# Moving token sums, normalisations and GpSimd's rows around the start of each block of a fused attention and gated-MLP kernel

## The chip, the cores and the metric

The kernel runs on one core of one Trainium2 chip. The metric is the device time of one execution in microseconds. The kernel before was timed three times; the median counts. The profile is of one further execution.

## The reference

Eight batches of 576 tokens with eight heads of 64 go through linear attention without a softmax, a norm per head, and a gated MLP on all 4608 tokens:

```python
kv = np.einsum('bhsd,bhse->bhde', k, v)
out = np.einsum('bhsd,bhde->bhse', q, kv)
x = out / sqrt(mean(out * out, -1) + 1e-6) * g_norm       # then laid out as 4608 x 512
g, val = x @ w_gate, x @ w_val                            # 512 x 1536 each
ffn_out = (gelu(g) * val) @ w_out                         # 1536 x 512
result = x + sigmoid(x @ w_res) * ffn_out
```

## The kernel before

**Blocks.** The work is cut into nine blocks, counted from 0. Blocks 0 to 7 hold 512 tokens of batch 0 to 7; block 8 holds the 64 tokens that remain of each batch (the "remainders", 512 together). For each block the MLP is computed from x transposed, `xT`, and attention for a later batch runs between its products: while block m is at work, batch m + 2 gets its `kv`, its heads' products, sums of squares and its norm.

**Products by seven instead of eight.** Blocks 2 to 8 compute the gate (u = `g`) and value (u = `v`) products by a scheme of Strassen's kind: each is split into quadrants, and seven products stand for eight. `gv_group` does it for 512 of the 1536 columns; a block has three groups (i = 0, 1, 2). The scheme needs four sums of `xT`'s quadrants per block, the *token sums* `ts` 0 to 3 (`token_sums`, on VectorE). Products 5, 6, 7 and 4 take sums 0, 1, 2 and 3. One product is four matmuls of 128x256. The output product with `w_out` has the same shape (`out_by_products`, its products `w`), and so has the one with `w_res` (`res_halves`).

**The order is written out by hand.** There is a string of words for a group, and each engine executes its own instructions in the order in which the words issue them:

```python
ORDERS = {
    None: "1g 1v Eg 5g 6g Ev 5v dg 6v dv Fg 2g Fv 2v 7g g11 7v cg 3g cv 3v h11 g12 4g g21 h12 4v g22 h21 h22",
    False: "1g 1v Eg 5g Ev 5v dg 6g dv 6v Fg 2g Fv 2v 7g g11 7v cg 3g cv 3v h11 g12 4g g21 h12 4v g22 h21 h22",
```

A digit with a letter is a product on TensorE: 1 opens bank A, 5 opens bank F; 6, then 7, then 4 add to A; 2 adds to E, 3 to F. `E` is a copy of A into bank E (ScalarE), ahead of which 6 may not add to A. `d` is a copy of F to SBUF (ScalarE). `F` and `c` are VectorE's sums A + d, ahead of which 7 (after `F`) and 4 (after `c`) may not add to A. `g11` to `g22` are Gelu on ScalarE; `h11`, `h12` and `h21` are the products gate times value on VectorE, `h22` on GpSimd. The first groups of blocks 2 to 6 take the order `None`, other groups `False`; the last of a block has a third one.

**Work hung between the words.** `at_word(blk, i, word, f)` executes f behind a word of group i of block blk. `aside_out(blk, key, f)` executes f at a place of the output product of block blk; the keys come in the order `D`, `F`, `00`, `22`, `01`, `11`, `end`. What the change and the prediction's steps touch:

- `a_norm`: twelve small steps on GpSimd that give `ny`, 1 / rms, at place `F` of the output.
- `a_t(b, i)`: the normalisation of a quarter of a batch, `t<-op,ny` (VectorE, from the heads' product in PSUM bank i of four); i = 4 (`NJ`) is the remainder, `t<-o,ny`, from SBUF.
- `d_xT`: the transpose of `t` to `xT` by DMA, on SP's queue. `d_rem_qT` and `d_qT` transpose the next queries on the same queue.
- `a_g`: `xT` times g, in place, on VectorE (`xT<-xT,gcol`).
- `pf`: an output quarter times the gate, `osb<-th,w..`, on VectorE, or on GpSimd for one quarter. The last, `osb<-th,wA`, frees the bank that the next block's value product takes as E.
- `row_times_g`: GpSimd multiplies the block's four rows of `t` by g (`t<-t,g`) once `t` is not needed without g; `fin` adds them to the output (`osb<-osb,t`), and `store` writes it. `hold` is a copy of one element that keeps GpSimd from going on until what it reads is there.

**Banks.** The eight PSUM banks rotate. The first group of a block takes as F of its gate and value the banks that hold the heads' products 0 and 1, and the second group takes 2 and 3 as A. So 5g, 5v of the first group and 1g, 1v of the second wait for `a_t` 0 to 3.

Of the kernel before, what the change touches and what calls it, by code (L numbers as in the profile page):

```python
# [18 lines left out]
def kernel(  # L19
# [15 lines left out]
    nc = tc.nc  # L35
    P = nc.NUM_PARTITIONS
    B, H, S, D = q.shape
# [567 lines left out]
    def out_by_products(blk, banks, amid):  # L605
# [103 lines left out]
        def others():  # L709


            prod(w["A"], s_[1], wo_t[:, 1], False)
            aside("F")
            sub(nc.vector, w["F"], w["A"], w["d"], ALU.add)
            if res_and_attn(blk):
                s_last(blk)
            aside("00")
            prod(w["E"], a_of(blk, 1, 2), b_of(2, 1), False)
            if not whole(blk + 1):
                pf((0, 0), w["E"])  # L720
            aside("22")
            prod(w["A"], s_[2], wo_t[:, 2], False)
            c22 = res_all[part((1, 1))]
            sub(nc.vector, c22, w["A"], w["d"], ALU.add)
            if whole(blk + 1):
                pf((0, 0), w["E"])
            aside("01")
            prod(w["F"], s_[3], b_of(2, 2), False)
            pf((0, 1), w["F"])
            aside("11")  # L730
            prod(w["A"], a_of(blk, 2, 2), wo_t[:, 3], False)
            if whole(blk + 1):
                pf((1, 1), c22, nc.gpsimd)
                pf((1, 0), w["A"])
                aside("end")
            else:
                pf((1, 1), c22)
                pf((1, 0), w["A"])
            if blk + 1 == WHOLE or blk + 1 == LAST[0]:
                nc.gpsimd.tensor_copy(out=hold, in_=x_sums[blk + 1][0:1, 3, 1, 1, 0:1])  # L740
            if blk == LAST[0]:
                nc.gpsimd.tensor_copy(out=hold, in_=s_[3][0:1, 0, 0:1])
            for j in range(NJ):
                row_times_g(blk, j, nc.gpsimd)
# [3 lines left out]
            rows_behind()  # L748

        def rows_behind():  # L750

# [144 lines left out]
    def token_sums(blk, eng):  # L896
# [12 lines left out]
        ]  # L909

    ORDERS = {
# [3 lines left out]
    }  # L915

    def gv_group(blk, g, banks, amid, order):

        if blk not in hids:
            hids[blk] = hidp.tile([P, NF, NJ * P], FP16, tag="hid", name="hid")  # L920
# [61 lines left out]
            eng = nc.gpsimd if q == "22" else nc.vector  # L982
            eng.tensor_tensor(out=dst, in0=ge[q], in1=source(q, "v"), op=ALU.mult)  # L983

        for word in ORDERS[order].split():
# [12 lines left out]
            for f in amid.get(word, ()):  # L998
                f()
# [359 lines left out]
    def plan_attn_2():  # L1359
# [13 lines left out]
            at(m, 9 + j // 2, lambda j=j: a_t(b, j))  # L1373
        at(m, 10, lambda: d_xT(b, 0, NJ))
        for i in range(2):
            aside_out(m, "F", lambda i=i: a_g(b, 2 * i, 2 * i + 2))

    WHOLE = 2
    GROUPS = {blk: (1, 2) for blk in range(2, WHOLE)} | {blk: (0, 1, 2) for blk in range(WHOLE, B - 1)} | {B - 1: (1, 0, 2), B: (0, 1, 2)}
# [9 lines left out]
    def plan_attn_ahead(b):  # L1389
# [25 lines left out]
            at(m, NF - 1, lambda: a_kv(b, act))  # L1415
            at(m, NF, lambda: load_behind(b))
        if rem:
            at_word(m + 2, 0, "cv", lambda: a_g(b, NJ, NJ + 1))
            own = 2 * pair(b) + 1 == b
            at_word(m, last, "5v" if own else "3g", lambda: a_rem_kv(b))  # L1420
            at_word(m, last, "dv" if own else "g12", lambda: kv_out(b))
            if own:
                at_word(m, last, "3g", lambda: rem_mm(b))
            at_word(m, last, "g12", lambda: rem_out(b))
        else:
            at(m, NF, lambda: a_o(b), lambda: a_ss(b, 0), lambda: a_ss(b, 1))
            aside_out(m, "D", lambda: a_ss(b, 2), lambda: a_ss(b, 3))
        aside_out(m, "F", lambda: a_norm(b, 0, NJ + rem, pool))
        first = [lambda: new_block(b), lambda: a_t(b, 0), lambda: a_t(b, 1)]
        if whole(m + 1):  # L1430
            aside_out(m, "01" if m + 1 == WHOLE else "11", *first[0:2])
            amid_out[m].setdefault("end", []).insert(0, first[2])
        else:
            at(m, NF + 3, *first)
        if whole(m + 1):
            t = [lambda j=j: a_t(b, j) for j in range(NJ)]
            if rem:
                at_word(m + 1, 0, "h21", lambda: a_t(b, NJ), lambda: d_xT(b, NJ, NJ + 1))
            for i, word, fs in (
                (0, "1v", t[2:3]),  # L1440
                (0, "Fv", [t[3], lambda: d_xT(b, 0, NJ)]),
                (1, "cv", [lambda: a_g(b, 0, 2)]),
                (2, "Fv", [lambda: a_g(b, 2, NJ)]),
            ):
                at_word(m + 1, i, word, *fs)
# [18 lines left out]
    for blk in GROUPS:  # L1464
        t = token_sums(blk, nc.vector)
        if blk == 2:
            aside_out(blk - 1, "00", *t[0:2])
            aside_out(blk - 1, "end", *t[2:4])
            continue
        for key, f in zip(("00", "00", "22", "01") if whole(blk) else ("00", "22", "01", "11"), t):  # L1470
            aside_out(blk - 1, key, f)
    wr_ = wr_sums(nc.vector)
    at(0, NF + 1, *wr_[0:3])
# [42 lines left out]
    for blk in range(B + 1):  # L1516
# [21 lines left out]
        else:  # L1538
            slots = [lambda f=f: m_gval(blk, f) for f in range(NF)]
            groups = GROUPS.get(blk, ())  # L1540
            if groups:
# [6 lines left out]
                def group(i, blk=blk, ends=ends):  # L1548
                    if i == 0:
                        ends.extend(banks_of(blk))  # L1550
                        if blk + 2 < B:
                            o = att_at[blk]
                            pattn.opening = o[2:] + o
                    order = None if i == 0 and whole(blk) else i == len(GROUPS[blk]) - 1
                    gv_group(blk, GROUPS[blk][i], ends[i], amid_gv.get((blk, i), {}), order)

                for i in range(len(groups)):
                    slots[n + GF * i] = lambda i=i: group(i)
# [77 lines left out]
```

## Time and profile before

| | |
|---|---|
| median of 3 runs | 321.47 us (321.26 to 323.02) |
| profiled execution, whole | 321.97 us |
| its span, first to last instruction | 320.2 us |
| TensorE busy | 311.9 us (97%) |
| VectorE busy | 274.6 us (86%) |
| ScalarE busy | 210.8 us (66%) |
| GpSimd busy | 187.2 us (58%) |
| start of block 2, 3, 4, 5, 6, 7 | 91.59, 124.82, 157.34, 189.87, 222.60, 253.37 us |

The starts are those of each block's first product in the timeline. Busy time is the union of an engine's instructions; the end of a matmul is modelled, so two products in a row overlap in the records, and the time between their starts tells more than their ends. A timeline line has the start and the length in us, the engine, the line of the kernel, the operation, what it writes and reads, and in brackets the idle time ahead of it with what ended it. `x4` merges instructions in a row.

### The profile page before, as it was taken

To read this page: it belongs to the slowest core of one execution; us is meant where nothing else is said; L and a number is where in the kernel's file an instruction comes from. 1 tells how busy PE (TensorE), PEld (TensorE's weight loads), DVE (VectorE), ACT (ScalarE), POOL (GpSimd) and SP (SyncE) were. 2 spreads that over 40 slices of the span, in tenths; PEclk is the share of its full clock that TensorE was granted. 3 is DMA by queue.
4 is the path that set the end of the run, shared out by engine and by line. 5 is a ranking of instruction groups with operands and counts; after the bars stand their busy time and mean duration, and the time that the engine had idled before them with its cause. 6 is when DMAs were issued, how large, how long until landed. Compare 5 with 4: busy or idle time off the path is not lost.

```text
span 320.2 us, 7756 instructions
## 1 busy us (share of the span) xinstructions
PE 311.9 (97%) x3044; PEld 247.5 (77%) x3044; DVE 274.6 (86%) x486; ACT 210.8 (66%) x385; POOL 187.2 (58%) x249
## 2 busy tenths in 40 slices
PE   8989999999999999999999999999999999999993
PEld 3544755444788888888888888888888888888882
DVE  5788889799888899989998999799988777897774
ACT  3673684465847795878587858795768467836760
POOL 2792350572869378757875777517761375396332
PEclk9999999999999999999999999999999999999998
DMA  8999999799994899479947894800340003001204
GB/s 251 328 204 204 195 204 190 168 155 178 176 106 82 199 130 105 82 215 120 112 82 217 109 124 69 227 6 0 69 147 2 0 3 134 0 2 44 89 2 131
DMA packets 76694, 38.90 MB, mean 122 GB/s; under 512 B 42098, under 2 KB 74354, under 8 KB 76658
## 3 DMA queue, kind: packets, MB, share of 16 engines
q0 software_dynamic: 38752, 17.17, 42.4%
q1 hardware_dynamic: 37328, 20.71, 25.3%
q8 instruction: 24, 0.39, 0.5%
q10 hardware_dynamic: 578, 0.52, 0.5%
q14 instruction: 12, 0.10, 0.1%
HBM read 38.80 MB, written 9.44 MB: 151 GB/s over the span
## 4 chain that ended last, share of the span: by engine, by line
PE 96%; DVE 2%; issue 0%; ACT 0%; DVEq 0%
PE Av L946 12%; PE Ag L946 12%; PE wA L515 12%; PE Fv L946 6%; PE Fg L946 6%; PE gps L410 5%; PE vps L410 5%; PE rA L566 4%; PE fps L447 3%; PE Ev L946 3%; PE Eg L946 3%; PE wD L515 3%; PE wF L515 3%; PE wE L515 3%; PE w L515 2%; PE idle L1111 2%
## 5 line engine op out<-in xcount | busy, mean ns | idle before, releaser
L983 POOL TENSOR_TENSOR hid<-ge,c 128x512 f16<-128x512 f16 x22 | 25.6, 1162 | 40.2 <-ACT ge L977 40.2
L515 PEld LDWEIGHTS <-hid_s 128*128 128x128 f16 x384 | 37.6, 98 | 4.5 <-issue 0.2
L946 PEld LDWEIGHTS <-wsv 128*128 128x128 f16 x352 | 34.0, 98 | 5.6 <-issue 1.3
L946 PEld LDWEIGHTS <-wsg 128*128 128x128 f16 x352 | 34.4, 98 | 4.1
L361 POOL TENSOR_TENSOR t<-t,g 128x512 f16<-128x512 f16 x32 | 37.1, 1189 | 0.0
L702 POOL TENSOR_TENSOR osb<-osb,t 128x512 f32<-128x512 f32 x28 | 34.0, 1244 | 0.0
L956 ACT COPY Eg<-Ag 128x512 f32<-128x512 f32 x22 | 12.9, 585 | 27.8 <-PE Ag L946 27.8
L515 PEld LDWEIGHTS <-hid 128*128 128x128 f16 x288 | 28.2, 98 | 3.5
L946 PEld LDWEIGHTS <-wg 128*128 128x128 f16 x264 | 25.8, 98 | 3.2
L946 PEld LDWEIGHTS <-wv 128*128 128x128 f16 x264 | 25.8, 98 | 3.0
L946 PE MATMUL Av<-ts,wsv 128*128 128x256 f16 x176 | 26.4, 272 | 0.2 <-ACT Ev L956 0.2
L946 PE MATMUL Ag<-ts,wsg 128*128 128x256 f16 x176 | 26.4, 273 | 0.0
L967 DVE TENSOR_TENSOR Fg<-Ag,d 128x512 f32<-128x512 f32 x22 | 15.3, 696 | 12.3 <-ACT d L960 7.6
L258 DVE TENSOR_REDUCE ss<-sq 128x8 f32<-128x512 f32 x32 | 20.5, 679 | 1.7 <-ACT sq L253 1.7
L398 ACT ACTIVATE ge<-gps 128x512 f16<-128x512 f32 x20 | 11.8, 599 | 14.2 <-PE gps L410 14.0
L515 PE MATMUL wA<-wo_ts,hid_s 128*128 128x256 f16 x168 | 20.6, 273 | 0.0
L977 ACT ACTIVATE ge<-Eg 128x512 f16<-128x512 f32 x22 | 13.2, 598 | 10.0 <-PE Eg L946 10.0
L977 ACT ACTIVATE ge<-c 128x512 f16<-128x512 f32 x22 | 13.8, 627 | 7.8 <-DVE c L967 7.8
L345 DVE TENSOR_TENSOR t<-op,ny 128x512 f16<-128x512 f32 x28 | 18.4, 684 | 0.5 <-POOL ny L319 0.4
L977 ACT ACTIVATE ge<-Fg 128x512 f16<-128x512 f32 x22 | 13.0, 591 | 8.6 <-PE Fg L946 6.6
L967 DVE TENSOR_TENSOR c<-Ag,d 128x512 f32<-128x512 f32 x22 | 15.2, 689 | 4.1 <-PE Ag L946 4.1
L410 PE MATMUL gps<-xT,wg 128*128 128x512 f16 x72 | 18.5, 379 | 0.0
(219 smaller groups left out, 860.2 us busy)
## 6 DMA issues: line engine op xcount, KB each, us to landing
out_dram<-osb SPq DMA_DIRECT2D x14, 512.0 KB, 3.6
qraw<-in_q_dram POOLq DMA_DIRECT2D x7, 512.0 KB, 6.8
k<-in_k_dram POOLq DMA_DIRECT2D x7, 512.0 KB, 8.7
v<-in_v_dram POOLq DMA_DIRECT2D x7, 512.0 KB, 10.5
wg<-in_moe_w_gate_dram POOLq DMA_DIRECT2D x2, 512.0 KB, 8.4
wv<-in_moe_w_val_dram POOLq DMA_DIRECT2D x2, 512.0 KB, 8.8
wo<-in_moe_w_out_dram POOLq DMA_DIRECT2D x2, 512.0 KB, 13.9
out_dram<-osb SPq DMA_DIRECT2D x4, 256.0 KB, 4.5
```

Of the source, the lines that this page charges most:

```text
L258: nc.vector.tensor_reduce(out=out_, in_=sqs.pop((b, i)), op=ALU.add, axis=mybir.AxisListType.X)
L345: nc.vector.tensor_tensor(out=t, in0=o, in1=scale, op=ALU.mult)
L361: eng.tensor_tensor(out=t_t[blk][:, jj, :], in0=t_t[blk][:, jj, :], in1=g16, op=ALU.mult)
L410: nc.tensor.matmul(ps[:, j0 * P : j1 * P], lhsT=w[:, cc, :], rhs=xT_t[blk][:, j0:j1, cc, :], start=(cc == 0 and j0 == 0), stop=(cc == NP - ...
L515: nc.tensor.matmul(ps[:, e - es[0], :], lhsT=a[:, f, e * P : (e + 1) * P], rhs=b[:, f, :], start=(start and e == es[0] and f == 0), stop=( ...
L566: nc.tensor.matmul(out_[:, e, :], lhsT=x_[:, e, cc, :], rhs=w_[:, cc, :], start=(first and e == 0 and cc == 0), stop=(cc == 1), skip_group ...
L702: nc.gpsimd.tensor_tensor(out=res_all[of], in0=res_all[of], in1=t_t[blk][of], op=ALU.add)
L946: nc.tensor.matmul(out_[:, r, :], lhsT=lhsT, rhs=rhs, start=(first and r == 0 and c == 0), stop=(c == 1), skip_group_check=True,)
L956: nc.scalar.copy(out=tile_of("E", u), in_=ps["A", u])
L967: nc.vector.tensor_tensor(out=dst, in0=ps["A", u], in1=sb["d", u], op=ALU.add)
L977: nc.scalar.activation(out=ge[q], in_=source(q, "g"), func=AF.Gelu)
L983: eng.tensor_tensor(out=dst, in0=ge[q], in1=source(q, "v"), op=ALU.mult)
```

## The change

It rearranges five things. The token sums of blocks 3 to 6: sum 2 goes behind the last output quarter of the block before, sum 3 behind the word `Fv` of the block's first group. First groups get the common order of words. In the output stage the first two normalisations stand together ahead of the last output quarter; the fourth goes from `Fv` to `cv` of the first group, with the transpose of `xT` behind it, and in block 2 the third goes from `1v` to `Fv` and the first multiplication by g in the second group from `cv` to `h21`. GpSimd's four rows in the output of blocks 2 to 5 are issued at `Fv` of the next block, behind a `hold` on sum 3. The multiplication by g of remainders leaves the first groups of blocks 4 to 7 (one row each) and becomes two of two rows in block 7. In block 1's output, `xT` times g goes from place `F` to place `00`, behind the sum `wF`.

```diff
-            if blk + 1 == WHOLE or blk + 1 == LAST[0]:
-                nc.gpsimd.tensor_copy(out=hold, in_=x_sums[blk + 1][0:1, 3, 1, 1, 0:1])
-            if blk == LAST[0]:
-                nc.gpsimd.tensor_copy(out=hold, in_=s_[3][0:1, 0, 0:1])
+            if WHOLE < blk + 1 < LAST[0]:
+                at_word(blk + 1, 0, "Fv", rows)
+            else:
+                rows()
+            rows_behind()
+
+        def rows():
+            sums = s_[3][0:1, 0, 0:1] if blk == LAST[0] else x_sums[blk + 1][0:1, 3, 1, 1, 0:1]
+            nc.gpsimd.tensor_copy(out=hold, in_=sums)
             for j in range(NJ):
                 row_times_g(blk, j, nc.gpsimd)
...
-        None: "1g 1v Eg 5g 6g Ev 5v dg 6v dv Fg 2g Fv 2v 7g g11 7v cg 3g cv 3v h11 g12 4g g21 h12 4v g22 h21 h22",
...
-            aside_out(m, "F", lambda i=i: a_g(b, 2 * i, 2 * i + 2))
+            amid_out.setdefault(m, {}).setdefault("00", []).insert(i, lambda i=i: a_g(b, 2 * i, 2 * i + 2))
...
-            at_word(m + 2, 0, "cv", lambda: a_g(b, NJ, NJ + 1))
+            if b + 1 == B:
+                for i, word in ((0, "cv"), (2, "Fv")):
+                    at_word(LAST[0], i, word, lambda b=B // 2 + i: a_g(b, NJ, NJ + 2))
...
-            aside_out(m, "01" if m + 1 == WHOLE else "11", *first[0:2])
-            amid_out[m].setdefault("end", []).insert(0, first[2])
+            aside_out(m, "11", *first)
...
-                (0, "1v", t[2:3]),
-                (0, "Fv", [t[3], lambda: d_xT(b, 0, NJ)]),
-                (1, "cv", [lambda: a_g(b, 0, 2)]),
+                (0, "Fv" if first_whole else "1v", t[2:3]),
+                (0, "cv", [t[3], lambda: d_xT(b, 0, NJ)]),
+                (1, "h21" if first_whole else "cv", [lambda: a_g(b, 0, 2)]),
                 (2, "Fv", [lambda: a_g(b, 2, NJ)]),
...
-        for key, f in zip(("00", "00", "22", "01") if whole(blk) else ("00", "22", "01", "11"), t):
+        if whole(blk):
+            aside_out(blk - 1, "00", *t[0:2])
+            aside_out(blk - 1, "end", t[2])
+            at_word(blk, 0, "Fv", t[3])
+            continue
+        for key, f in zip(("00", "22", "01", "11"), t):
...
-                    order = None if i == 0 and whole(blk) else i == len(GROUPS[blk]) - 1
-                    gv_group(blk, GROUPS[blk][i], ends[i], amid_gv.get((blk, i), {}), order)
+                    gv_group(blk, GROUPS[blk][i], ends[i], amid_gv.get((blk, i), {}), i == len(GROUPS[blk]) - 1)
```

`first` is the new block's tiles, `a_t(b, 0)` and `a_t(b, 1)`; `first_whole` is true where m + 1 is block 2.

More of the change, by code (lines that the diff above doesn't have):

```diff
@@ L747, in others @@
                     row_times_g(B, p, nc.gpsimd)
-            rows_behind()
         def rows_behind():
@@ L915, with gv_group @@
     }
-    def gv_group(blk, g, banks, amid, order):
+    def gv_group(blk, g, banks, amid, last):
         if blk not in hids:
@@ L983, in hidden @@
             eng.tensor_tensor(out=dst, in0=ge[q], in1=source(q, "v"), op=ALU.mult)
-        for word in ORDERS[order].split():
+        for word in ORDERS[last].split():
             if word[0].isdigit():
@@ L1438, in plan_attn_ahead @@
                 at_word(m + 1, 0, "h21", lambda: a_t(b, NJ), lambda: d_xT(b, NJ, NJ + 1))
+            first_whole = m + 1 == WHOLE
             for i, word, fs in (
-                (0, "1v", t[2:3]),
-                (0, "Fv", [t[3], lambda: d_xT(b, 0, NJ)]),
-                (1, "cv", [lambda: a_g(b, 0, 2)]),
+                (0, "Fv" if first_whole else "1v", t[2:3]),
+                (0, "cv", [t[3], lambda: d_xT(b, 0, NJ)]),
+                (1, "h21" if first_whole else "cv", [lambda: a_g(b, 0, 2)]),
                 (2, "Fv", [lambda: a_g(b, 2, NJ)]),
```

## The prediction

> **What bounds the kernel now.** I read the page's parts 1 and 4 first, then the table of windows with one window per block, then the timelines of single groups, engine by engine. Blocks are counted from 0; a block starts at S, its first product of a first group.
>
> ```profile
> PE 311.9 (97%) x3044; PEld 247.5 (77%) x3044; DVE 274.6 (86%) x486; ACT 210.8 (66%) x385; POOL 187.2 (58%) x249
> ...
> PE 96%; DVE 2%; issue 0%; ACT 0%; DVEq 0%
> ```
>
> TensorE holds the end: 96% of the chain is its own work. Its instruction lists hold the same instructions before and after, so only its waits can change. Beyond 90 us I compared each product's start with the one before: a group of four matmuls (a "product") goes every 0.437 us, one of twelve every 1.31. The late ones are the stock that the change can gain from.
>
> ```profile
> 158.21 0.60 PE L946 MATMUL Fg<-ts,wsg 128*128 128x256 f16 x4
> 158.65 0.60 PE L946 MATMUL Ag<-ts,wsg 128*128 128x256 f16 x4
> 159.26 0.60 PE L946 MATMUL Fv<-ts,wsv 128*128 128x256 f16 x4
> ...
> 95.25 0.60 PE L946 MATMUL Ag<-ts,wsg 128*128 128x256 f16 x4
> 95.85 0.60 PE L946 MATMUL Av<-ts,wsv 128*128 128x256 f16 x4
> ...
> 106.79 0.60 PE L946 MATMUL Av<-ts,wsv 128*128 128x256 f16 x4 [0.20 <-ACT Ev L956]
> ```
>
> - Block 4, first group: 5v (Fv) starts 0.61 after 6g instead of 0.44, so 0.17 late. Blocks 3, 5 and 6 have the same at 126.74, 191.79 and 224.56 (0.17, 0.18, 0.17): 0.70 in all.
> - Block 2, first group: 95.25 to 95.85 is 0.60, and with 93.38, 95.25 and 97.63 it is 0.37 in all. Last group: 6v waits for ACT's Ev at 106.79; with 105.54 and 108.63 it is 0.51.
> - Block 1's output: a product of twelve starts at 86.19, the next at 87.67, 1.48 instead of 1.31: 0.17.
>
> Together **1.75 us** (0.54%) is all that the touched stretches can give back. A measurement of this kernel tells about 0.5%, 1.6 us, from no change.
>
> VectorE, ScalarE and GpSimd around the start of block 4:
>
> ```profile
> 156.44 0.49 POOL L318 TENSOR_SCALAR nh<-nh 128x40 f32<-128x40 f32 x1
> 157.02 0.27 POOL L319 TENSOR_TENSOR ny<-nh,ny 128x40 f32<-128x40 f32 x1
> ...
> 157.93 0.68 DVE L698 TENSOR_TENSOR osb<-th,wA 128x512 f32<-128x512 f32 x1
> 158.53 1.28 DVE L345 TENSOR_TENSOR t<-op,ny 128x512 f16<-128x512 f32 x2
> 159.81 0.70 DVE L967 TENSOR_TENSOR Fg<-Ag,d 128x512 f32<-128x512 f32 x1
> ...
> 158.70 0.57 ACT L956 COPY Ev<-Av 128x512 f32<-128x512 f32 x1
> 159.18 0.59 ACT L960 COPY d<-Fg 128x512 f32<-128x512 f32 x1
> ```
>
> 5v waits for the second normalisation (the first of the two at 158.53, ending 159.21): its bank held that head product. Ev starts 0.09 after osb<-th,wA ends, since it takes that bank. VectorE has no gap here.
>
> **What the skill says.** "SBUF — State Buffer", Who interferes with whom: a VectorE instruction with two SBUF inputs, or in a 2-port mode, and a GpSimd instruction that reads SBUF exclude each other for a whole instruction, and the earlier to issue wins; with one SBUF input VectorE doesn't contend. The trace agrees on the exclusion:
>
> ```profile
> 164.59 1.16 POOL L983 TENSOR_TENSOR hid<-ge,c 128x512 f16<-128x512 f16 x1 [1.61 <-ACT ge L977]
> 164.96 1.33 DVE L345 TENSOR_TENSOR t<-o,ny 128x512 f16<-128x512 f32 x1
> 166.22 0.69 DVE L967 TENSOR_TENSOR Fg<-Ag,d 128x512 f32<-128x512 f32 x1
> ...
> 103.40 1.49 DVE L370 TENSOR_SCALAR xT<-xT,gcol 128x1024 f16<-128x1024 f16 x1
> ...
> 103.45 1.15 POOL L702 TENSOR_TENSOR osb<-osb,t 128x512 f32<-128x512 f32 x1
> ```
>
> The remainder's normalisation t<-o (two SBUF inputs) ends 0.55 after the GpSimd instruction that it met (165.75), in block 3 too. Sums from PSUM (Fg, c, t<-op) keep 0.68 to 0.70 beside GpSimd. On who wins, the trace adds a warning: at 103.40 g on xT, recorded 0.05 ahead of GpSimd's next add, lost to it and ended 0.28 after that add's end (104.61).
> "Perfetto Trace Analysis", Identifying the Most-Contended Engine, holds matmul busy time to be a poor measure; hence the products' starts above.
>
> **The change, part by part.** Read with block 4; blocks 3, 5 and 6 repeat its times to some 0.02.
>
> 1. *Sums 2 and 3 leave the output stage.* Beside them two of GpSimd's small steps for ny took 0.49 and 0.32, where the like take 0.29 or less and 0.24. So ny comes 0.3 earlier, at 157.0 instead of 157.29. Bounds: 0 (VectorE was not the cause) and 0.45, where osb<-th,wF (at 156.25 then) holds the first normalisation.
> 2. *Both normalisations ahead of osb<-th,wA.* At VectorE's step of 0.60: t 157.0 and 157.6, wA's at 158.2. The second t ends at 158.3, ahead of 5v's new turn (158.65): the 0.17 goes. Late next is Ev: 158.2 + 0.68 + 0.09 = 158.97, ending 159.54. In the common order 6v follows 6g, its turn is S + 5 x 0.437 = 159.52, and with 0.05 from ScalarE to TensorE it starts at 159.59, 0.07 late. Then d (ends 0.505 after Ev), Fg at 160.08, Fv 160.68 to 161.37, so 7v at 161.42 against its turn of 161.27: **0.15 late in place of 0.17**, a draw. Bounds, from step 1's: 0 and 0.45.
> 3. *Third sum at the last output, fourth behind Fv, t 3 behind cv, no g on the remainder.* VectorE loses 0.34 x 2 earlier and gets it here, less the g (0.26). The sums are needed by 7g and 4g, whose turns are later than their ends (159.2, 161.7). t 3 ends at 163.5; 1v of the next group, its first user, is due at 164.0. The transpose of xT moves with it from 161.88 to about 163.6 on SP; at the 4.3 to landing of the page it is there at 168, g on it follows at about 169. The remainder's transpose, qrT and qT behind it on SP move by under 1 us; their users are at 174 and later.
> 4. *GpSimd's rows behind the fourth sum*, four of 1.15 (1.11 apart), with one more 0.18 hold per block. They start 3.5 later; hid (h22) of the group ends at 167.9 instead of 165.75, for c of the next group needs it by 168.2, so it stays hidden. The four adds and the stores behind them move by 2 us; the next hid is used at 176.9. Queued behind the hold are only these.
> 5. **Where rows and t<-o meet.** The fourth sum starts 0.60 after Fv, 161.28, and ends at 161.70. Behind it VectorE has c, c, t, three hid: t<-o's turn is 0.34 + 6 x 0.597 = 3.92 after the sum's start, 165.20. GpSimd: hold 0.06 after the sum, first row 0.15 later (both as at 94.06), the fourth 3.34 after that: 165.25; the third ends at 165.29. This is the pattern of 103.40, 0.05 ahead and lost. I take it as lost: the fourth row ends at 166.41, t<-o at 166.96, Fg of the second group runs 166.88 to 167.57, 7g starts at 167.62 against a turn of S + 22 x 0.4366 = 166.95; Fv ends at 168.16, 7v starts at 168.21 against 167.38. The block is then **0.83 late**, 0.66 more than now. Both chains hang on the same sum, so the four blocks should agree: 4 x 0.66 = +2.6. Bounds for t<-o itself: 0.69 (free) and 1.7 (a whole row, and 0.55).
> 6. *Block 2 and block 1's output.* With g on xT behind wF, wF reads A at 86.55 instead of 86.92: -0.17. The first group gets its two t early, Ev ends before 6v's turn: -0.37, with about 0.03 left at 4v. With g on xT behind h21 in the second group, h12 comes 1.4 earlier and so does Ev of the last: -0.51. Sum **-1.0**.
> 7. *Block 7.* g on 1024 elements twice for 512 once: 0.48 against 0.34 at cv, and 0.48 in the last group at Fv, where VectorE idles 0.45 ahead of c. TensorE had no late product there, VectorE 1.1 idle in the second group: nothing.
>
> Sum: -1.0 + 2.6 = +1.6. The profiled execution took 321.97 (span 320.2 and 1.8 around it), so 323.6 on its scale; it lies 0.5 above the median of 321.47, on whose scale I forecast **323.1**.
>
> **Rivals.**
> - *t<-o gets the port after the third row.* It then ends at 165.84, the fourth row waits instead, and 7g has 0.4 to spare. For it: the record puts t<-o 0.05 ahead, and the skill lets the earlier one win. Against it: 103.40. First groups -0.1, block 2 -1.0: **320.4**, not slower. It decides at 0.05: anything that makes t<-o 0.1 earlier against the rows.
> - *Lost, and ny no earlier.* Ev, the sum and t<-o all come 0.3 later against TensorE: 0.3 x 4 more, **324.3**. Against it: the 0.49 beside a sum.
> - *Port won and ny earlier by 0.4.* No late product is left in first groups: -1.0 - 0.7, **319.8**.
> - *The change doesn't do what it says*: the order of instructions shows every move, so this has no share.
>
> **Numbers.** Lost port 0.48 (322.5 to 323.7; a little over half lies above 323.08, since stalls not seen can only add), lost with late ny 0.21, won 0.23, won and all gone 0.08. Slower by over 0.5%: 0.27 + 0.21 = 0.48; faster 0.08; within 0.44. The range reaches from the won case to the late one, 320.1 to 324.4.
>
> **What would show it.** t<-o of 1.7 in blocks 3 to 6 and 7g of the second group about 0.5 late: step 5 right; t<-o of 0.7: the first rival. 6v late by under 0.1: step 2. ny at S - 0.3: step 1. No late product in 85 to 110 us: step 6. A late first product of a group, or hid on GpSimd holding c, would make the reading wrong.

## The result, and the profile after

The changed kernel takes **354.41 us** (median of 4 runs, 354.07 to 356.27), against 321.50 us for the kernel before on the same chip. The ratio is **1.102 (95% interval 1.098 to 1.107)**: 33 us slower, where 1.6 were forecast. The profiled execution took 354.48 us, with a span of 352.5.

The page of the kernel after: busy times, the granted TensorE clock in 40 slices, the chain by engine, and two groups of part 5 (busy time, mean ns of one, idle time ahead and what ended it).

```profile
PE 320.7 (91%) x3044; PEld 251.5 (71%) x3044; DVE 298.0 (85%) x484; ACT 210.0 (60%) x385; POOL 184.0 (52%) x253
...
PEclk9999999999999997899969999699978999999999
...
PE 78%; DMA 10%; issue 7%; DVE 1%; SPq 1%; POOL 0%; DVEq 0%
...
L950 PE MATMUL Ag<-ts,wsg 128*128 128x256 f16 x176 | 28.1, 285 | 23.6 <-DVE Fg L971 23.6
...
L345 DVE TENSOR_TENSOR t<-o,ny 128x512 f16<-128x512 f32 x4 | 29.2, 7292 | 0.0
```

The clock line of the kernel before:

```profile
PEclk9999999999999999999999999999999999999998
```

Four instructions t<-o take 7.29 us each (1.33 to 1.58 before), TensorE stands 23.6 us before `Ag` for `Fg`, and its clock, full before, dips at four places. The same in one block, the timelines of VectorE, GpSimd and TensorE in block 3:

```profile
131.22 7.29 DVE L345 TENSOR_TENSOR t<-o,ny 128x512 f16<-128x512 f32 x1
...
127.92 4.49 POOL L361 TENSOR_TENSOR t<-t,g 128x512 f16<-128x512 f16 x4
132.38 1.15 POOL L987 TENSOR_TENSOR hid<-ge,c 128x512 f16<-128x512 f16 x1
133.49 4.47 POOL L702 TENSOR_TENSOR osb<-osb,t 128x512 f32<-128x512 f32 x4
...
132.68 0.60 PE L950 MATMUL Ev<-xT,wv 128*128 128x256 f16 x4
139.18 1.01 PE L950 MATMUL Ag<-ts,wsg 128*128 128x256 f16 x4 [5.89 <-DVE Fg L971]
139.98 1.06 PE L950 MATMUL Av<-ts,wsv 128*128 128x256 f16 x4
```

t<-o stands until GpSimd's adds end (137.96) and ends 0.55 behind them, at 138.51. `Fg` follows, and 7g starts at 139.18 instead of 133.12, 6.06 late. From there to 144.0 a product of four takes 0.85 instead of 0.44: 23 matmuls take 4.81 us where they would take 2.51, 2.3 us more.

| block, start to start | 2 | 3 | 4 | 5 | 6 | 7 |
|---|---|---|---|---|---|---|
| before, us | 33.23 | 32.52 | 32.53 | 32.77 | 30.74 | 30.57 |
| after, us | 32.37 | 40.94 | 40.96 | 41.19 | 39.04 | 30.81 |
| difference | -0.86 | +8.42 | +8.43 | +8.42 | +8.30 | +0.24 |

The differences add up to 32.95, about the whole result: four blocks that each lose 6.06 + 2.3, and small change beside them. (The trace before has the start of block 6 at 222.64, 0.04 later than in the list of starts further up.)

The first group of block 4 and the last of block 2 in the kernel after, to set against those shown in the prediction:

```profile
165.97 0.60 PE L950 MATMUL Ag<-ts,wsg 128*128 128x256 f16 x4
166.55 0.60 PE L950 MATMUL Av<-ts,wsv 128*128 128x256 f16 x4
...
167.86 0.60 PE L950 MATMUL Ag<-ts,wsg 128*128 128x256 f16 x4
168.39 0.60 PE L950 MATMUL Av<-ts,wsv 128*128 128x256 f16 x4
...
104.91 0.60 PE L950 MATMUL Ag<-ts,wsg 128*128 128x256 f16 x4
105.35 0.60 PE L950 MATMUL Av<-ts,wsv 128*128 128x256 f16 x4
```

In block 4, 6v starts 0.58 after 6g instead of 0.44 and 7v 0.53 after 7g: 0.14 and 0.09 late. In block 2, 6v follows 6g by 0.44, where it was 0.37 late before.

### The profile page after: what moved, and what is told of

Read it like the earlier page. It is cut to its first block, busy times and chain, and to the rows that moved or that the text cites. A ratio compares the mean times of both kernels' runs of the same rounds, so it can differ in the third digit from the quotient of the medians.

```text
span 352.5 us, 7758 instructions
## 1 busy us (share of the span) xinstructions
PE 320.7 (91%) x3044; PEld 251.5 (71%) x3044; DVE 298.0 (85%) x484; ACT 210.0 (60%) x385; POOL 184.0 (52%) x253
## 4 chain that ended last, share of the span: by engine, by line
PE 78%; DMA 10%; issue 7%; DVE 1%; SPq 1%; POOL 0%; DVEq 0%
PE Ag L950 12%; PE Av L950 11%; PE wA L515 10%; PE Fv L950 6%; PE Fg L950 6%; DMA wo<-in_moe_w_out_dram 4%; PE rA L566 4%; PE gps L410 3%; PE fps L447 3%; PE vps L410 3%; PE wE L515 3%; PE wD L515 3%; PE wF L515 3%; DMA wg<-in_moe_w_gate_dram 3%; PE w L515 2%
## 5 line engine op out<-in xcount | busy, mean ns | idle before, releaser
L950 PEld LDWEIGHTS <-wsg 128*128 128x128 f16 x352 | 35.6, 102 | 29.5 <-issue 24.3
L950 PE MATMUL Ag<-ts,wsg 128*128 128x256 f16 x176 | 28.1, 285 | 23.6 <-DVE Fg L971 23.6
L950 PEld LDWEIGHTS <-wsv 128*128 128x128 f16 x352 | 35.7, 102 | 6.8 <-issue 0.3
L702 POOL TENSOR_TENSOR osb<-osb,t 128x512 f32<-128x512 f32 x28 | 31.4, 1147 | 0.0
L950 PEld LDWEIGHTS <-wg 128*128 128x128 f16 x264 | 26.7, 101 | 4.1
L950 PEld LDWEIGHTS <-wv 128*128 128x128 f16 x264 | 26.6, 101 | 3.8
L345 DVE TENSOR_TENSOR t<-o,ny 128x512 f16<-128x512 f32 x4 | 29.2, 7292 | 0.0
L950 PE MATMUL Av<-ts,wsv 128*128 128x256 f16 x176 | 28.2, 286 | 0.0
```

Of the source, the lines that this page charges most:

```text
L345: nc.vector.tensor_tensor(out=t, in0=o, in1=scale, op=ALU.mult)
L702: nc.gpsimd.tensor_tensor(out=res_all[of], in0=res_all[of], in1=t_t[blk][of], op=ALU.add)
L950: nc.tensor.matmul(out_[:, r, :], lhsT=lhsT, rhs=rhs, start=(first and r == 0 and c == 0), stop=(c == 1), skip_group_check=True,)
```

## The experiments

At the start stood two theories. One: GpSimd keeps VectorE out for as long as its instructions that read SBUF follow each other, a *run* (here rows, hid and adds). The other: a waiting t<-o is let in at the next end of a GpSimd instruction if it was asked well before that end, and here it came a trifle too late each time. Every edit but one is made to the kernel after. "Asked 0.3 ahead" means that the recorded start of the VectorE instruction lies 0.3 us before that of GpSimd's next.

### A break in the run, and an earlier asking

`gap` puts a memset of one element behind the fourth row. `t_at_h12` issues t<-o one place, 0.6 us, earlier.

```diff
             for j in range(NJ):
                 row_times_g(blk, j, nc.gpsimd)
+            if WHOLE < blk + 1 < LAST[0]:
+                nc.gpsimd.memset(spare, 0.0)
...
-                at_word(m + 1, 0, "h21", lambda: a_t(b, NJ), lambda: d_xT(b, NJ, NJ + 1))
+                at_word(m + 1, 0, "h12", lambda: a_t(b, NJ), lambda: d_xT(b, NJ, NJ + 1))
```

> The changed kernel with one GpSimd memset of a single element, which reads nothing, behind the fourth row of blocks 2 to 5. Port theory (what starves t<-o is that each next GpSimd instruction that reads SBUF already stands at the port): the memset leaves the port free for a moment, t<-o is served behind the fourth row, about 1.8 us long, TensorE about 0.6 late in each block, about 323.7 us. Rival (GpSimd keeps the port as long as it is busy at all, or t<-o waits for something else): t<-o stays at 7.3 us and the time at 354.

> The changed kernel with the remainder's normalisation t<-o (and its transpose) at the word h12 instead of h21 of the first group: it asks for the port one VectorE step, 0.60 us, earlier, about 0.64 ahead of the fourth row's start, in the middle of the third row. Handover theory (an instruction that asks within some 0.05 us of the change from one GpSimd instruction to the next loses to every GpSimd instruction that follows without a gap; one that asks in the middle of an instruction is served at its end): t<-o takes about 1.2 us, no long wait of TensorE, no half clock, about 321.7 us. Rival, the run (t<-o loses to the whole run of rows, hid and adds whenever it meets it, whatever the moment): t<-o takes about 7.9 us and the time stays at 354 or above.

Measured: gap **324.19 us**, t_at_h12 **357.07** (one execution each, the kernel before 322.89). VectorE, GpSimd and TensorE in block 3 of gap:

```profile
131.81 1.73 DVE L345 TENSOR_TENSOR t<-o,ny 128x512 f16<-128x512 f32 x1
...
132.94 0.09 POOL L752 MEMSET spare<- 1x1 f32 x1
133.00 1.57 POOL L989 TENSOR_TENSOR hid<-ge,c 128x512 f16<-128x512 f16 x1
...
134.21 0.60 PE L952 MATMUL Ag<-ts,wsg 128*128 128x256 f16 x4 [0.33 <-DVE Fg L973]
134.81 0.60 PE L952 MATMUL Av<-ts,wsv 128*128 128x256 f16 x4
```

A memset of 0.09 in each of four blocks takes back 30 of the 33 us. t<-o gets in at 132.94, hid waits for it (1.57 instead of 1.15), and TensorE's clock does not dip. 7g and 7v start 0.50 and 0.16 late; with the 0.23 of the first group the block is 0.89 late, where the forecast had 0.83 (and 1.7 for t<-o) for a row lost *once*. The first t<-o of t_at_h12:

```profile
131.14 7.90 DVE L345 TENSOR_TENSOR t<-o,ny 128x512 f16<-128x512 f32 x1
```

It is asked 0.64 ahead of the fourth row, as are the other three, and all take 7.9: asked well inside a row t<-o still loses the run, so the second theory falls in this form.

### Other times of asking

`rows_later` makes GpSimd's copy ahead of the rows once to four times more in blocks 3 to 6, `t_later` puts one to four VectorE memsets ahead of t<-o, `scan` mixes both for places between.

```diff
-            nc.gpsimd.tensor_copy(out=hold, in_=sums)
+            for _ in range(blk if WHOLE < blk + 1 < LAST[0] else 1):          # rows_later
+                nc.gpsimd.tensor_copy(out=hold, in_=sums)
...
-                at_word(m + 1, 0, "h21", lambda: a_t(b, NJ), lambda: d_xT(b, NJ, NJ + 1))
+                at_word(m + 1, 0, "h21", *[lambda: nc.vector.memset(spare, 0.0)] * (b - 3), lambda: a_t(b, NJ), lambda: d_xT(b, NJ, NJ + 1))   # t_later
...
+            for kind in {3: "hhm", 4: "hhmm", 5: "m", 6: "mm"}.get(blk + 1, ""):  # scan: h the copy, m a memset
+                if kind == "h":
+                    nc.gpsimd.tensor_copy(out=hold, in_=sums)
+                else:
+                    nc.gpsimd.memset(spare, 0.0)
...
-                at_word(m + 1, 0, "h21", lambda: a_t(b, NJ), lambda: d_xT(b, NJ, NJ + 1))
+                at_word(m + 1, 0, "h21", *[lambda: nc.vector.memset(vspare, 0.0)] * (3 if b > 4 else 0), lambda: a_t(b, NJ), lambda: d_xT(b, NJ, NJ + 1))
```

> The changed kernel with 1, 2, 3 and 4 further hold copies ahead of the rows in blocks 3, 4, 5 and 6, which move the rows and all behind them about 0.24 us later for each; t<-o then asks about 0.29, 0.53, 0.77 and 1.0 us ahead of the fourth row. Handover theory: served at the third row's end, about 0.87, 1.11, 1.35 and 1.6 us long, about 321.5 us. Rival, the run: 7.5 to 8.3 us each, 354 or above.

> The changed kernel with 1, 2, 3 and 4 memsets of a single element on VectorE ahead of t<-o in blocks 3, 4, 5 and 6, some 0.06 us each (they write one element and read nothing), so t<-o asks about 0.02, 0.08, 0.14 and 0.2 us behind the recorded start of the fourth row. Handover theory: block 3 still starves (7.2 us) or is served once; blocks 5 and 6, and likely 4, are served at the fourth row's end, about 1.6 us; about 330 us or 323. Rival, the run: about 7.2 us in all four, 354.

> The kernel after with t<-o's asking set to four places within a running row: block 3 about 0.54 us after the start of the third row, block 4 about 0.49 after it (GpSimd's rows begin later by two copies of one element and one or two memsets), block 5 about 0.27 and block 6 about 0.21 after the start of the fourth row (three VectorE memsets ahead of t<-o, one or two GpSimd memsets ahead of the rows). Theory C, a request is kept only if it is made late enough in the running instruction (third row: 0.47 lost and 0.59 was served; fourth row: 0.20 lost and 0.32 was served): each of the four is either served at the next end (block 3: 1.1 to 1.2 us; block 5: 1.4) or lost for the whole run (7 to 8 us), later ones served and earlier ones lost, block 3 more likely served than 4 and 5 more than 6. Rival D, the outcome has nothing to do with the time of asking within the row: no order, for instance block 4 served and block 3 lost. The total is about 321.5 plus 8.4 for each that is lost.

Measured: 339.13, 347.05 and 329.77 us, one execution each. (In scan block 4 got the three VectorE memsets too, so t<-o was asked 0.67 after the third row's start there, not 0.49.) The twelve t<-o of these traces, with the time by which they were asked ahead of GpSimd's next instruction:

| GpSimd's next | asked ahead, us: t<-o took, us |
|---|---|
| fourth row | 0.28: 0.86; 0.44: 1.02; 0.52: 1.10; 0.54: 1.12; 0.77: 8.02; 0.99: 8.23; 0.04: 7.29 |
| hid | 0.79: 1.37; 0.92: 7.05; 0.95: 7.08; 1.03: 7.17; 1.08: 1.67 |

Each is let in at the first end after it was asked, or not until GpSimd idles; nothing lies between. Each lost run costs some 8.4 us of the total. From 0.28 to 0.54 ahead all were let in, from 0.77 most were lost, but not in order (0.79 and 1.08 were let in): the rule that `scan` was to test, that only the time of asking decides, does not hold at its long end.

### A break too early, and other kinds of instruction

`open_row4` puts the memset ahead of the fourth row instead of behind it. `kind` puts one more VectorE instruction at t<-o's place (`h21`), ahead of it, of another kind in each block.

```diff
+                if j + 1 == NJ and WHOLE < blk + 1 < LAST[0]:                    # open_row4
+                    nc.gpsimd.memset(spare, 0.0)
                 row_times_g(blk, j, nc.gpsimd)
...
+        if b == 4:                                                               # kind, blocks 3 to 6
+            nc.vector.tensor_tensor(out=out, in0=g16, in1=g16, op=ALU.add)
+        elif b == 5:
+            nc.vector.tensor_scalar(out=out, in0=g16, scalar1=gcol, scalar2=None, op0=ALU.mult)
+        elif b == 6:
+            nc.vector.tensor_tensor(out=out, in0=o, in1=o, op=ALU.add)
+        elif b == 7:
+            nc.vector.tensor_tensor(out=out[:, 0:256], in0=o[:, 0:256], in1=o[:, 256:512], op=ALU.add)
```

> The kernel after with one GpSimd memset of one element ahead of the fourth row in blocks 3 to 6. Theory A, GpSimd keeps the port as long as its instructions that read SBUF follow each other, and a memset between them opens it: t<-o asks about 0.1 us ahead of the row, is served at the memset, takes 0.65 to 0.9 us instead of 7.29, 7g of the second group is at most 0.1 late and TensorE's clock does not dip. What is left of the change is then block 2 (-0.86), first groups (0.23 instead of 0.17, +0.06 four times) and block 7 (+0.24): 321.5 - 0.4 = 321.1. Theory B, a memset opens the port only for a request that was already waiting when it began: t<-o comes 0.05 too late for it, loses to the row and all that follows, 7.2 us, and the time is 354.

> The kernel after with one more VectorE instruction ahead of t<-o, so asked for 0.04 ahead of the fourth row, another kind in each block: block 3 a sum of two fp16 tiles of 128x512 in SBUF (as a token sum), block 4 an fp16 tile times a column (as g on xT), block 5 a sum of fp32 and fp32 without broadcast, block 6 the same on 128x256. It fills t's remainder, which t<-o then overwrites. Theory E, whether a VectorE instruction loses a run depends on the time of asking alone: all four take over 7 us, as t<-o did there. Theory F, it depends on the kind (in the runs so far fp16 sums and g on xT lost one GpSimd instruction at most): the fp16 ones of blocks 3 and 4 take 1.4 to 1.6 us, the fp32 ones of blocks 5 and 6 over 7. In either case t<-o behind it meets the rest of the run and may lose it.

Measured: open_row4 **348.15 us** (346.72 to 354.04), kind 355.71. In open_row4 the memset begins 0.01 to 0.03 after t<-o's recorded start, and t<-o loses the run in three of four blocks of the trace (7.32 to 7.33; in the fourth it is let in behind the fourth row, 1.76). The recorded start of t<-o overlaps the end of the instruction before it by 0.08, so it may not have been waiting yet (not shown). The timeline of VectorE in kind, the inserted instruction of each block:

```profile
131.35 7.03 DVE L351 TENSOR_TENSOR t<-g 128x512 f16<-128x512 f16 x1
...
173.03 6.89 DVE L353 TENSOR_SCALAR t<-g,gcol 128x512 f16<-128x512 f16 x1
...
214.29 7.30 DVE L355 TENSOR_TENSOR t<-o 128x512 f16<-128x512 f32 x1
...
255.84 7.02 DVE L357 TENSOR_TENSOR t<-o 128x256 f16<-128x256 f32 x1
```

An fp16 sum, a product with a column (one SBUF tile as input, as g on xT), an fp32 sum and one of half the length lose alike: it is no property of t<-o.

The same trace shows something else. `Fg` of block 7's last group, in the kernel after and in kind:

```profile
300.47 0.70 DVE L971 TENSOR_TENSOR Fg<-Ag,d 128x512 f32<-128x512 f32 x1 [1.73 <-PE Av L950]
...
301.69 0.70 DVE L983 TENSOR_TENSOR Fg<-Ag,d 128x512 f32<-128x512 f32 x1 [1.36 <-ACT d L976]
```

Both kernels have the remainders' g of two rows at the same places. But in kind `Fg` does not wait for 6v, no product is late, and block 7 takes 30.57 as in the kernel before, not 30.81.

### Moving the meeting elsewhere

`hold2` makes GpSimd's copy twice in all four blocks, so that t<-o is asked 0.28 ahead. `t_first` moves t<-o to `Fv`, ahead of the rows, and `t_first_g` also restores the remainders' g.

```diff
+            for _ in range(2 if WHOLE < blk + 1 < LAST[0] else 1):               # hold2
                 nc.gpsimd.tensor_copy(out=hold, in_=sums)
...
-                at_word(m + 1, 0, "h21", lambda: a_t(b, NJ), lambda: d_xT(b, NJ, NJ + 1))   # t_first
+                at_word(m + 1, 0, "h21", lambda: d_xT(b, NJ, NJ + 1))
...
-            at_word(blk, 0, "Fv", t[3])
+            at_word(blk, 0, "Fv", t[3], lambda b=blk + 1: a_t(b, NJ))
...
-            if b + 1 == B:                                                        # t_first_g
-                for i, word in ((0, "cv"), (2, "Fv")):
-                    at_word(LAST[0], i, word, lambda b=B // 2 + i: a_g(b, NJ, NJ + 2))
+            at_word(m + 2, 0, "cv", lambda: a_g(b, NJ, NJ + 1))
```

> The kernel after with the copy of one element ahead of GpSimd's rows made twice in blocks 3 to 6, so that rows begin 0.24 us later and t<-o is asked for 0.28 ahead of the fourth row. Theory A (the loss of the whole change is t<-o's lost run): served at the third row's end in all four blocks, 0.86 us as in one block of an earlier run, 7g on time; the time is that of the kernel before less block 2 (0.86), plus 0.06 in each of four first groups and 0.24 in block 7: 321.5 - 0.4 = 321.1. Rival: the outcome is chance from block to block; at least one block loses its run, 8.4 us each, 329 or more.

> The kernel after with t<-o moved from h21 to Fv of the first group, behind the fourth token sum and ahead of both c, so that it is asked for before GpSimd's first row begins; its transpose stays at h21. Theory A: t<-o takes 0.6 to 0.8 us, the first row waits for it, c comes 0.6 later, which 4g and 4v have spare, 7g of the second group is on time; 321.1, as without the loss. Rival: the first row is asked first (hold ends early) and t<-o loses four rows, hid and adds, with c behind it: 4g over 5 us late, 350 or more.

> As the one before, and the multiplication by g of the remainders as in the kernel before (one row in the first groups of blocks 4 to 7, at cv). If block 7's 0.24 (7g and 7v of its last group late) comes from the two-row form at Fv, there is no late product at block 7's last group and the time is 0.24 below that of the kernel without this edit: 320.9, close to the 320.7 of block 2's part alone. Rival: block 7's loss has another cause and stays, 321.1.

Measured: hold2 **347.35 us**, but from **328.64 to 355.03** over six executions; t_first **340.89** (ratio 1.059, 1.057 to 1.062); t_first_g **360.91** (1.121, 1.118 to 1.124). The four t<-o of hold2's profiled execution, its shortest:

```profile
131.17 7.53 DVE L345 TENSOR_TENSOR t<-o,ny 128x512 f16<-128x512 f32 x1
171.36 0.86 DVE L345 TENSOR_TENSOR t<-o,ny 128x512 f16<-128x512 f32 x1
203.95 0.86 DVE L345 TENSOR_TENSOR t<-o,ny 128x512 f16<-128x512 f32 x1
236.78 0.86 DVE L345 TENSOR_TENSOR t<-o,ny 128x512 f16<-128x512 f32 x1
```

All four are asked 0.27 to 0.28 ahead. Three are let in and one is not, at a lead that `rows_later` had shown served. The other executions were not traced; at 8.4 us each their times fit runs lost in two to four blocks, and their mean granted clock is lower too (0.960 to 0.975, against 0.989 here and 0.961 in the kernel after). So the outcome seems to change by chance from block to block and from one execution to the next. None of the three forecasts of some 321 us came true.

In t_first, t<-o is free (0.68), though 4g and 4v of the first group, which I had expected to have its time spare, are 0.38 late. The loss moves on to the next VectorE instruction that meets a run, g on xT in the second group, which loses two adds and hid:

```profile
135.27 4.47 DVE L370 TENSOR_SCALAR xT<-xT,gcol 128x1024 f16<-128x1024 f16 x1
...
136.92 0.60 PE L950 MATMUL Fg<-ts,wsg 128*128 128x256 f16 x4
140.39 0.82 PE L950 MATMUL Fv<-ts,wsv 128*128 128x256 f16 x3 [2.87 <-DVE hid L987]
```

5v of the second group starts 3.04 late, and 1.6 more go to the slow clock behind it. In t_first_g the same happens in block 3, and in blocks 4 to 6 the remainder's g at `cv` loses the whole run, 9.08 us at 167.89, 8.7 late on TensorE. Moving one instruction out of a run's way puts another into it.

### Part 4 undone, part 6 alone, and the rest

`rows_now` (and `rows_now5`, the same kernel with more executions) issues the rows in the output stage as before the change, without the copy ahead; all else stays. `rows_now_g` also restores the remainders' g. `mend2` is the kernel *before* with the block 2 part alone.

```diff
-            if WHOLE < blk + 1 < LAST[0]:                                         # rows_now
-                at_word(blk + 1, 0, "Fv", rows)
-            else:
-                rows()
+            rows()
...
-            nc.gpsimd.tensor_copy(out=hold, in_=sums)
+            if not WHOLE < blk + 1 < LAST[0]:
+                nc.gpsimd.tensor_copy(out=hold, in_=sums)
...
-            aside_out(m, "F", lambda i=i: a_g(b, 2 * i, 2 * i + 2))               # mend2, to the kernel before
+            amid_out.setdefault(m, {}).setdefault("00", []).insert(i, lambda i=i: a_g(b, 2 * i, 2 * i + 2))
...
+            aside_out(m, "11", *first[0:2])
+            if m + 1 == WHOLE:
+                aside_out(m, "11", first[2])
...
+                (0, "Fv" if m + 1 == WHOLE else "1v", t[2:3]),
+                (0, "cv" if m + 1 == WHOLE else "Fv", [t[3], lambda: d_xT(b, 0, NJ)]),
+                (1, "h21" if m + 1 == WHOLE else "cv", [lambda: a_g(b, 0, 2)]),
...
-                    order = None if i == 0 and whole(blk) else i == len(GROUPS[blk]) - 1
+                    order = None if i == 0 and whole(blk) and blk > WHOLE else i == len(GROUPS[blk]) - 1
```

> The kernel after with part 4 alone undone: GpSimd's rows are issued in the output stage again, without a hold, and the sums 2 and 3 stay in their new places. Theory A (a VectorE instruction with two SBUF inputs can lose to a whole row of GpSimd instructions): t<-o meets only hid again and takes 1.3 us; but now sum 2 (asked about 1.5 after the block's start) and sum 3 (about 4 after it) fall in the four rows, which run from about 1.1 to 5.5 after the start. Sum 2 takes 1 to 4 us instead of 0.34, Fg behind it and 7g are late by up to 3 us in each of blocks 3 to 6: 325 to 335. Rival, the loss belongs to t<-o and the adds alone (a sum is short and slips in between two rows): sums of at most 1.4 us, 321 to 323.

> The kernel of the run that undid part 4 alone, now with enough runs for an interval. Its one run gave 322.51, with 1.40 us of it at one place in the opening where the others lose 0.1. If all 33 us hang on part 4 (GpSimd's rows behind the fourth sum), the median is 321.2: block 2's -0.86, first groups 0.30 in place of 0.17 (+0.13 four times), block 7 +0.25. Rival: sums 2 and 3, which now meet the rows with 0.47 and 0.37 to the next row, lose a run by chance in some executions, and the runs spread by several us, as those with a lead of 0.28 did.

> As the one before, and the multiplication by g of the remainders as in the kernel before (one row at cv in the first groups of blocks 4 to 7). If block 7's 0.25 hangs on the two-row form, no late product is left there and the time is 0.25 less, 320.9. Against it: g at cv of a first group then meets GpSimd's rows; in an earlier run with rows behind the fourth sum such a g lost 8.7 us in three blocks. Here the rows are done by about 5.7 us after the block's start and g is asked for at about 6.3, so it should meet nothing, and c and hid behind it are 0.26 later, up to 0.1 late at 7g: 320.9 to 321.3. Rival: it still loses a run somewhere, 329 or more.

> The kernel before with the block 2 part of the change alone (step 6 of the prediction: g on xT behind wF in block 1's output, both normalisations and the third ahead or at the new places, the common order in block 2's first group). If that part stands alone, no late product between 85 and 110 us and 0.86 less, as block 2 of the kernel after is shorter: 320.6. Rival, block 2's gain is taken back in block 3, since GpSimd's and ScalarE's own due times set the start of it: block 2 is 0.86 shorter, block 3 that much longer, 321.5.

Measured: rows_now 322.51 (one execution); rows_now5 **321.74 us**, ratio **1.0006** (0.9991 to 1.0022), 321.2 to 323.6 over 14 executions, so without part 4 the change is a draw; rows_now_g **324.37**, 1.0076 (1.0056 to 1.0095); mend2 **320.71**, **0.9962** (0.9947 to 0.9977). VectorE and GpSimd around the start of block 3 in rows_now5:

```profile
125.20 0.78 DVE L478 TENSOR_TENSOR ts<-xT 128x512 f16<-128x512 f16 x1
...
127.70 0.69 DVE L478 TENSOR_TENSOR ts<-xT,ts 128x512 f16<-128x512 f16 x1
...
124.55 4.86 POOL L361 TENSOR_TENSOR t<-t,g 128x512 f16<-128x512 f16 x4
```

The sums now meet the rows and take 0.78 and 0.69 instead of 0.41, let in each time at the next row's end; that first group is 0.30 late. My first expectation for this kernel, sums of 1 to 4 us, was wrong. In rows_now_g block 7's late products are gone, as expected, but t<-o comes later by the 0.26 of g and now begins 0.07 behind an add: it waits for that add, 1.63 to 1.64 in blocks 4 to 6, and 7g and 7v are 0.80 and 0.16 late. For the 0.24 of block 7, three blocks pay about 1 us each.

### A break at every end

`memsets` puts a memset behind each row and ahead of each add of blocks 3 to 6; `hold2_memsets` does so in hold2.

```diff
                 row_times_g(blk, j, nc.gpsimd)
+                if WHOLE < blk + 1 < LAST[0]:
+                    nc.gpsimd.memset(spare, 0.0)
...
             of = part(jj)
+            if WHOLE < blk + 1 < LAST[0]:
+                nc.gpsimd.memset(spare, 0.0)
             nc.gpsimd.tensor_tensor(out=res_all[of], in0=res_all[of], in1=t_t[blk][of], op=ALU.add)
```

> The kernel after with a GpSimd memset of one element behind each row and ahead of each add of blocks 3 to 6, so that no two GpSimd instructions that read SBUF follow each other there. Theory A, a memset lets in a VectorE instruction that is waiting when it starts: t<-o is asked about 0.13 ahead of the memset behind the third row, takes 0.75 us, or at worst 1.9 at the next; no block loses a run, all executions lie within 1 us, 321.1 to 323.5. Rival G, whoever loses the first end waits for an idle GpSimd, memset or not (the memset 0.02 after the asking did not help in three of four blocks): t<-o over 7 us, 350.

> As the one before, with the copy ahead of the rows made twice, so that t<-o is asked about 0.37 ahead of the memset behind the third row. Without the memsets this kernel gave 328.6 to 355.0 from run to run: chance decides in each block. Theory A: the memset takes the chance away, t<-o 0.95 us in every block, all executions within 1 us, 321.1 to 321.4. Rival G: the spread stays, several us from run to run.

Measured: memsets **321.54 us** (320.80 to 323.29, 14 executions), ratio **0.9993** (0.9974 to 1.0012); hold2_memsets **321.62** (321.01 to 323.02), 1.0000 (0.9985 to 1.0015). The list of t<-o in memsets and in hold2_memsets (shortest, median and longest in ns, first and last start), and GpSimd in block 3 of memsets:

```profile
L345 DVE TENSOR_TENSOR t<-o,ny x4: 683/690/695, 131.1 to 229.1; 128x512 f16<-128x512 f32 x4
...
131.16 0.09 POOL L754 MEMSET spare<- 1x1 f32 x1
131.21 1.57 POOL L361 TENSOR_TENSOR t<-t,g 128x512 f16<-128x512 f16 x1
```

```profile
L345 DVE TENSOR_TENSOR t<-o,ny x4: 925/929/931, 131.1 to 229.1; 128x512 f16<-128x512 f32 x4
```

Every t<-o is let in at the first memset, and the fourth row waits instead. Nothing else of the order or the work was changed, and 32.9 us are gone: the loss was the run. hold2's spread of 26 us shrinks to 2.0, as wide as that of the kernel before, measured beside it (321.25 to 323.35); the 1 us that I had expected was too narrow for either. Why a memset lets VectorE in is less sure: it reads nothing from SBUF, but a short instruction that does read was not tried in its place.

## Why the prediction was wrong, point by point

1. *ny 0.3 earlier*: right. ny ends 0.30 ahead of block 3's first product, and the first normalisation starts 0.27 ahead, 0.07 later than reckoned.
2. *Both normalisations ahead of osb<-th,wA*: the mechanism was right (5v on time, Ev and then 7v late), the size short: 0.23 late where 0.15 was forecast (0.17 before). 6v was 0.14 late where 0.07 stood, which fits the 0.07 of step 1; 7v another 0.09.
3. *Sums, the third normalisation and the transpose moved*: hidden, as forecast; no late product in a first group but those two.
4. *GpSimd's rows behind the fourth sum*: costed at nothing, for hid and the adds still come in time. For GpSimd's own work that holds. What was not asked is what the four rows do directly ahead of hid and the adds. Before, the rows ended about 1.6 us ahead of hid (its bracket at 164.59, shown in the prediction, has that idle time); now six instructions follow the third row without a pause.
5. ***Where rows and t<-o meet*: the step that failed.** The timing came out to the hundredth: t<-o was asked about 0.04 ahead of the fourth row and lost to it. The bound of 1.7 us for t<-o did not hold. The step counted one lost GpSimd instruction, as at 103.40 of the kernel before, where g on xT lost one add. But that case could not tell one instruction from a whole run. The adds and the next hid there:

```profile
100.11 4.50 POOL L702 TENSOR_TENSOR osb<-osb,t 128x512 f32<-128x512 f32 x4
105.14 1.17 POOL L983 TENSOR_TENSOR hid<-ge,c 128x512 f16<-128x512 f16 x1 [0.54 <-ACT ge L977]
```

The lost add was the last of the four, and GpSimd idled for 0.54 us behind it. The Trainium skill, "SBUF — State Buffer", Who interferes with whom, says that whoever issues first has the shared ports for its whole instruction while the other is blocked, and the same page, Summary: rules for kernel authors, that the second to issue blocks until the first finishes; neither speaks of instructions that follow. The runs showed 7.29 us, six instructions, and gap confirmed the price for one loss (1.73 for t<-o, the block 0.89 late).

The second term of the step that was missing is the clock: a TensorE that stands still for 6 us comes back at half speed. The Trainium skill, "TensorE: Matmul & The Clock Gate", What's actually happening, has it: after an idle window of about 3.4 us the clock halves until a busy window has passed. The trace agrees: matmuls of 256 columns start 0.213 apart instead of 0.109 for 4.8 us, and the granted clock there is 0.50; that is 2.3 us per block. In t_first a start only 3.04 late was enough, a little less than the page's figure.

The block is thus 0.23 + 6.06 + 2.3 = 8.59 late where 0.83 stood. That is 8.42 more than before where 0.66 more was forecast, and 33.6 in the four blocks where 2.6 stood.

6. *Block 2 and block 1's output*: right. In the kernel after the late product of block 1's output is gone (-0.17), and block 2 is 0.86 shorter: -1.03 for -1.0 forecast. Alone (mend2) block 2 is 0.85 shorter in the trace, and the medians differ by 1.25 us.
7. *Block 7*: costed at nothing, and 0.24 late: 7g 0.08 and 7v 0.16 in the last group, where Fg waits until 6v ends. rows_now_g and t_first_g, without the g of two rows, have no late product there; but neither have kind and t_later, which keep it and have other VectorE instructions added in blocks 3 to 6. So it does not hang on that g alone, and why Fg starts later was not found.

That the kernel would be slower, and at which meeting, was foreseen; what a loss there costs was not. None of the rivals held either. All of them priced a loss at one row, and the range had no room for a second lost row (1.11 us) in each of four blocks. The profile before had no case that spoke for more: the one VectorE instruction that lost an end there, beyond the opening, lost the last of its run.

## What to carry to other kernels

Cost a meeting of VectorE and GpSimd on SBUF not by the instruction it meets but by the whole run of GpSimd instructions up to its next pause, and add the slow clock if TensorE idles some 3 us for it. When a profile shows one loss, look whether it was the last instruction of its run before taking it as the price. Before moving GpSimd work, look at what it will now touch on both sides: joining two short runs into a long one can cost by itself, though each part has time to spare. Where such a run can't be avoided on the way of a critical VectorE instruction, a one-element memset between its instructions (0.05 us of start-to-start time each here) can break it: with one at each end no t<-o lost a run here (memsets, hold2_memsets). Of all kernels run here the one before with the block 2 part alone is the fastest, 0.4% under the kernel before.

## What the runs showed of the hardware that was not expected

- A VectorE instruction that is not let in at the first end of a GpSimd instruction was, with one exception, not let in until GpSimd idled or issued a memset. From block 2 on the 18 traces have 36 such instructions: 31 waited until GpSimd idled, four got in at the memset of gap, and one, in open_row4, at the second end.
- Whether it is let in at the first end is settled neither by the time of asking nor by the kind of VectorE instruction. In the 16 traces without memsets at every end, from block 2 on, 112 of 113 that were asked 0.1 to 0.6 us ahead of the next GpSimd instruction were let in, 29 of 33 at 0.6 to 0.75, 23 of 34 beyond that, and none of 16 below 0.1. Many of these are the same place seen again: 16 of the 23 are `osb<-th,osb` at the start of block 8, asked 1.05 ahead of a row and let in in each trace. At the same lead of 0.64, t<-o lost the run in four of four in t_at_h12, and g on xT was let in in four of four in gap. What decides is open. One of each, from the kernel before and from gap:

```profile
284.40 1.63 DVE L698 TENSOR_TENSOR osb<-th,osb 128x512 f32<-128x512 f32 x1
...
136.12 0.97 DVE L370 TENSOR_SCALAR xT<-xT,gcol 128x1024 f16<-128x1024 f16 x1
```

- A memset must come while VectorE waits: 0.08 to 0.09 after t<-o's recorded start (memsets) it let t<-o in in four of four blocks, 0.01 to 0.03 after it (open_row4) in none of four.
